# Another way to the first block's decay factors, and other queues for the first loads, in a fused scan and feed-forward kernel

## The chip, the cores and the metric

The kernel runs on one core of one Trainium2 chip. Times are device microseconds (us) of one execution of the whole kernel; the time before is 124.99 us, the median of three runs (124.52 to 125.14). The engines are PE (TensorE), DVE (VectorE), ACT (ScalarE) and POOL (GpSimd); SP (SyncE) issues transfers. Each engine takes its instructions in the order in which the program gives them. SP, ACT and POOL each have a queue of transfers (DMA).

## What is computed

A chunked linear recurrence (a state-space layer with 4 batches, 8 heads, 768 tokens, 32 channels and a state of 16) is followed by a bilinear feed-forward layer:

```python
for c in range(nc):                       # chunks of the sequence
    cum = np.cumsum(log(a)[chunk])
    L = np.exp(cum_i - cum_j) * causal    # i >= j
    M = np.einsum('bhin,bhjn->bhij', Cc, Bc) * L
    y = M @ xc + (Cc @ state) * np.exp(cum)
    state = np.exp(sum(la)) * state + sum_j(Bc xc * exp(cum_last - cum_j))
out = ((y @ w_a) * (y @ w_b)) @ w_out     # 256 -> 1536 -> 256, 3072 tokens
```

## The kernel before

**Tiling.** The sequence is cut into 6 blocks of 128 tokens, and the 4 batches into 2 groups of 2 (`bt` counts the batches in a group), so there are 12 pairs of block and group; pair `p` is block `p // 2`, group `p % 2`. In the first four pairs a partition holds two neighbouring tokens (64 partitions for each of the two batches); later pairs hold one token on each partition. For a pair, B and C are scaled by decay factors (`scale_bc`, tiles bm and cm), turned by PE (`transposes`), multiplied into scores (`scores`), masked by `causal` (`mask`, L426), multiplied with x (`pv_u`, `pv`) and then sent through the feed-forward units: PE multiplies by Wa and Wb into the banks aps and bps, ACT copies aps to asb (L639), DVE multiplies bps by asb into hk (L646), and PE multiplies hk by Wo (ops).

**The decay factors.** `a` lies in `a_sb` on 32 partitions (batch and head) by block and token. `scan` (L234) runs a product along the 128 tokens of a block into Pr. The factor of a token is that product over the product at the block's middle, token 63: `over_mid` (L238) takes the reciprocal of the middle into rmid. C is scaled by the factor and B by its inverse. For block 0 `first_factors` (L241) scales Pr by rmid into Pe and turns it, 32 partitions by 64 columns at a time, into fC on 128 partitions, four turns; f0 (L761) takes the reciprocal into fB, and the scaling of B and C of pair 0 follows on DVE (L763, L764). The factors of the other blocks come later and in other ways. The products at the ends of the blocks (`hr`, L830, from Pr and rmid) carry the state from block to block.

**The order.** It is written out by hand (`manual_schedule`): the order of the calls is the order on each engine and each queue. At the start:

- SP issues a (L183), then B of pair 0's first batch, half of the C of that batch, the small table ch, half of the x of that batch, x of pair 1's first batch (x1), and the table c32. x1 is made to wait for f0 (L762).
- ACT issues B and C of pair 0's second batch, the other half of the first batch's C, x of the second batch and the other half of the first batch's x; behind these it loads its function table (L195).
- POOL clears the tile warm (L196), makes ident by a select (L205), makes both halves of causal by a select each (L208 to L212), and then issues B and C of pair 1 (four transfers), the first halves of Wa (two transfers), x of pair 1's second batch, and the first halves of Wb (two transfers). Its next work is the scaling of B and C of pair 1 (L778, L783), and then the second halves of Wa and Wb.
- DVE sets constants with memsets, waits for a, and makes the factors.
- PE runs multiplications without use (`warmup`) until the first transposes.

PE's first feed-forward units come at L801 (Wa) and L823 (Wb); the masks of pair 1 lie between them, pv of pair 1 after the first four matmuls with Wb. `times(0, 0)` (L829) is the first product into hk; hr, hs and hsx (L830 to L837) stand between it and `times(0, 1)`.

Of the kernel before, what the change touches and what calls it, by code (L numbers as in the profile page):

```python
# [10 lines left out]
f32 = mybir.dt.float32  # L11
# [3 lines left out]
ALU = mybir.AluOpType  # L15
# [14 lines left out]
def kernel(  # L30
# [13 lines left out]
    nc = tc.nc  # L44

    nb, H, S, D = x.shape
    N = B.shape[-1]
    Q = 128
# [5 lines left out]
    BH = nb * H  # L54
    NBP = nb // 2
    NP = NBP * NBLK
    NG = NBLK - 1
# [19 lines left out]
    causal = const.tile([128, 2, Q], f16, name="causal")  # L77
# [5 lines left out]
    big = ctx.enter_context(tc.tile_pool(name="big", bufs=1))  # L83
    a_sb = big.tile([BH, NBLK, Q], f32, name="a_sb")
    zero = big.tile([BH, Q], f32, name="zero")
# [11 lines left out]
    Pr = big.tile([BH, NBLK, Q], f32, name="Pr")  # L97
    rmid = big.tile([BH, NBLK], f32, name="rmid")
    NE = P0 // NBP
    fB = big.tile([128, NE, 2, NBP, H], f32, name="fB")  # L100
    fC = big.tile([128, NE, H + 4 * NBP * H], f32, name="fC")
    Pe = big.tile([BH, 2, 64], f32, name="Pe")
    selr = big.tile([BH, 2, NBP, H], f32, name="selr")
    NL = NBLK - P0 // NBP
    Ps = big.tile([BH, NL, Q], f32, name="Ps")
# [2 lines left out]
    hr = big.tile([BH, NG], f32, name="hr")  # L108
# [34 lines left out]
    def by_token(t_):  # L143
        return t_.rearrange("p h r n -> p (h r n)").rearrange("p (t h n) -> p t h n", t=2, h=H)

    def load1(eng, p, which, bt, i0=0, n=64):
        blk, bp = divmod(p, NBP)
        if p >= P0:
            return eng.dma_start(
                by_token(pair_in[p][which])[:, bt],  # L150
                (B, C, x)[which][2 * bp + bt, :, blk * Q : (blk + 1) * Q, :].rearrange("h q n -> q h n"),
            )
        src = (B, C, x)[which][2 * bp + bt, :, blk * Q + 2 * i0 : blk * Q + 2 * i0 + 2 * n, :]
        return eng.dma_start(
            pair_in[p][which][64 * bt + i0 : 64 * bt + i0 + n].rearrange("i h r n -> i h (r n)"),
            src.rearrange("h (i r) n -> i h (r n)", r=2),
        )
# [10 lines left out]
    def load_w(W, t, f=None):  # L168
        src = (moe_w_a if W is Wa else moe_w_b).rearrange("(f p) e -> p f e", p=128)[:, :, t * KC : (t + 1) * KC]
        fs = slice(0, 2) if f is None else slice(f, f + 1)  # L170
        return nc.gpsimd.dma_start(W[t][:, fs], src[:, fs])
# [12 lines left out]
    for p_ in range(3):  # L184
        tiles(p_)
    load1(nc.scalar, 0, 0, 1)
    load1(nc.sync, 0, 0, 0)
    load1(nc.scalar, 0, 1, 1)
    load1(nc.sync, 0, 1, 0, 0, 32)
    nc.sync.dma_start(ch, ph_t.ap())  # L190
    load1(nc.scalar, 0, 1, 0, 32, 32)
    load1(nc.scalar, 0, 2, 1)
    load1(nc.sync, 0, 2, 0, 0, 32)
    load1(nc.scalar, 0, 2, 0, 32, 32)
    nc.scalar.preload_act_table_set("natural_log_exp_and_others")  # L195
    nc.gpsimd.memset(warm.bitcast(u32), 0)  # L196
    nc.vector.memset(ident, 1.0)
    nc.vector.memset(causal, 1.0)
    nc.vector.memset(zero, 0.0)
    nc.vector.memset(hsx, 0.0)  # L200
    nc.vector.memset(causal_q, 1.0)
    nc.vector.memset(c32, 0.0)
    x1 = load1(nc.sync, 1, 2, 0)
    nc.sync.dma_start(c32[0:BH], p32_t.ap())
    nc.gpsimd.affine_select(  # L205
        out=ident, in_=ident, compare_op=ALU.is_equal, fill=0.0, base=0, pattern=[[-1, 128]], channel_multiplier=1
    )
    for bt in range(2):  # L208
        v = causal[64 * bt : 64 * bt + 64]
        nc.gpsimd.affine_select(  # L210
            out=v, in_=v, compare_op=ALU.is_ge, fill=0.0, base=0, pattern=[[-1, 2], [1, Q]], channel_multiplier=-2
        )  # L212
    for w in range(2):
        for bt in range(2):
            load1(nc.gpsimd, 1, w, bt)
    load_w(Wa, 0, 0)
    load_w(Wa, 0, 1)
    load1(nc.gpsimd, 1, 2, 1)
# [3 lines left out]
    def warmup(n, bank, reps=4):  # L222
        for _ in range(n):
            nc.tensor.matmul(
                bank[:, 0 : 128 * reps],
                warm,
                warm.unsqueeze(1).broadcast_to((128, reps, 128)),
                start=True,
                stop=True,
                skip_group_check=True,  # L230
            )


    def scan(lo, hi):  # L234
        for k in range(lo, hi):
            nc.vector.tensor_tensor_scan(Pr[:, k], a_sb[:, k], zero, 1.0, ALU.mult, ALU.add)

    def over_mid(lo, hi):  # L238
        nc.vector.reciprocal(rmid[:, lo:hi], Pr[:, lo:hi, 63])

    def first_factors():  # L241
        nc.vector.tensor_scalar(Pe, Pr[:, 0].rearrange("p (i r) -> p r i", r=2), rmid[:, 0:1], None, ALU.mult)
        for bt in range(2):
            for c in range(2):
                p0 = 64 * bt + 32 * c
                nc.vector.transpose(  # L246
                    fC[p0 : p0 + 32, 0, H - H * bt : H - H * bt + 64], Pe[:, :, 32 * c : 32 * c + 32]
                )

    def second_sel():  # L250
        nc.vector.tensor_scalar(
# [390 lines left out]
    def times(p, k2, b_ps, asb):  # L642
        s = st[p]
        if "hk" not in s:
            s["hk"] = ffh.tile([128, NK, 2 * Q], f16, name="hk", tag="hk")
        nc.vector.tensor_tensor(  # L646
            out=s["hk"][:, 2 * k2 : 2 * k2 + 2, :].rearrange("p k q -> p (k q)"), in0=b_ps, in1=asb, op=ALU.mult
        )
# [104 lines left out]
    def pull(p):  # L753
# [1 line left out]
            st[p].update(st.pop(("S", p)))  # L755

    warmup(11, SC[3])
    scan(0, 1)
    over_mid(0, 1)
    first_factors()  # L760
    f0 = nc.vector.reciprocal(fB[:, 0, :, 0], f_c(0)[:, :, 0])  # L761
    tc.add_manual_dep(x1.ins, f0.ins.name, AFTER, reason="x of pair 1 behind x of pair 0")  # L762
# [24 lines left out]
        out=causal_q, in_=causal_q, compare_op=ALU.is_ge, fill=0.0, base=0, pattern=[[1, Q]], channel_multiplier=-1  # L787
# [30 lines left out]
    for bt in range(2):  # L818
# [8 lines left out]
    units_mm(0, range(3), Wb, bps, 1, range(6))  # L827
    nc.scalar.copy(maskbd, headm.unsqueeze(2).broadcast_to((128, H, D)))
    times(0, 0, bps[0], asb[0])  # L829
    nc.vector.tensor_tensor(out=hr, in0=Pr[:, 0:NG, Q - 1], in1=rmid[:, 0:NG], op=ALU.mult)  # L830
    nc.vector.tensor_tensor(out=hs, in0=hr, in1=Pr[:, 1:NBLK, 63], op=ALU.mult)
    nc.vector.tensor_tensor(
        out=hsx[0:BH],
        in0=hs.unsqueeze(1).broadcast_to((BH, nb, NG)),
        in1=selb.rearrange("p (b g) -> p b g", b=nb),
        op=ALU.mult,
# [243 lines left out]
```

## Time and profile before

| What | Value |
|---|---|
| median of three runs | 124.99 us (124.52 to 125.14) |
| the profiled execution | 125.11 us |
| its span, first to last instruction | 123.4 us |
| PE busy | 117.3 us (95%) |
| DVE busy | 91.0 us (74%) |
| ACT busy | 75.7 us (61%) |
| POOL busy | 61.2 us (50%) |
| granted clock of PE | 1.000 |

The transfers at the start, by issue and time to landing (from the answers of the trace for short stretches; B, C and x of a pair come in one transfer for each batch, 64 KB for B and C and 128 KB for x, or in halves of these):

| Transfer | Queue | Issued at, us | Landed after, us |
|---|---|---|---|
| a | SP | 0.79 | 2.1 |
| B of pair 0, second batch | ACT | 0.79 | 2.5 |
| B of pair 0, first batch | SP | 1.24 | 3.0 |
| C of pair 0, second batch | ACT | 1.54 | 3.1 |
| C of pair 0, first batch, half | SP | 2.01 | 2.9 |
| B of pair 1, first batch | POOL | 2.21 | 3.3 |
| ch | SP | 2.65 | 3.0 |
| x of pair 0, second batch | ACT | 2.93 | 4.6 |
| B of pair 1, second batch | POOL | 3.08 | 3.7 |
| x of pair 0, first batch, half | SP | 3.34 | 4.0 |
| x of pair 0, first batch, other half | ACT | 3.58 | 4.1 |
| Wa, first piece | POOL | 5.12 | 5.1 |
| x of pair 1, first batch | SP | 5.21 | 6.6 |
| c32 | SP | 5.86 | 6.1 |
| x of pair 1, second batch | POOL | 6.20 | 6.1 |
| Wb, first piece | POOL | 6.91 | 6.2 |

Busy shares are averages over the span. A chain of waits is followed back from the last instruction, at each step to what released it. A line of the timeline gives start and duration, the engine, the line of the code, what is written from what, the shapes, how many instructions are merged, and in brackets how long the engine had been idle and what ended that.

### The profile page before, as it was taken

Reading aid. Unit: us, or ns where it says so; the run is one execution under the profiler, and the core shown is the slowest. Engines: PE = TensorE matmul, PEld = TensorE weight load, DVE = VectorE, ACT = ScalarE, POOL = GpSimd, SP = SyncE. Lnnn points to the kernel's source line nnn. Section 1 sums busy time; section 2 is a strip of 40 time slices with the busy share of each in tenths; the row PEclk is TensorE's granted clock in tenths of the full one; section 3 lists DMA queues with packets and bytes.
Section 4 is the critical chain, followed back from the end, with each engine's and each line's share of the span. In section 5 each row is a group of like instructions: output and inputs, shape, how many; then the busy total and the mean of one; then the engine's idle time right before and its main releaser. Section 6 shows DMA issues by size and latency. Waiting matters only on the chain.

```text
span 123.4 us, 3704 instructions
## 1 busy us (share of the span) xinstructions
PE 117.3 (95%) x1456; PEld 80.0 (65%) x1456; DVE 91.0 (74%) x182; ACT 75.7 (61%) x158; POOL 61.2 (50%) x88
## 2 busy tenths in 40 slices
PE   6799799999999999999999999999999999999990
PEld 2345669889898798744477465757464775555890
DVE  3999598973995979799986988996889544747200
ACT  0447846837669866987669767457637746657220
POOL 7997989099492994097996970056000000000000
PEclk9999999999999999999999999999999999999999
DMA  3999999978899989799977601011101012010122
GB/s 66 195 155 210 185 198 204 164 137 77 89 125 115 108 111 103 91 118 93 129 271 169 204 5 45 5 43 45 43 0 43 5 43 88 0 48 0 43 85 85
DMA packets 56401, 12.15 MB, mean 99 GB/s; under 512 B 51168, under 2 KB 55936, under 8 KB 56384
## 3 DMA queue, kind: packets, MB, share of 16 engines
q1 hardware_dynamic: 51808, 7.43, 36.3%
q0 software_dynamic: 2304, 4.06, 17.4%
q10 hardware_dynamic: 2272, 0.43, 1.8%
q8 instruction: 11, 0.18, 0.6%
q14 instruction: 6, 0.05, 0.1%
HBM read 11.13 MB, written 3.15 MB: 116 GB/s over the span
## 4 chain that ended last, share of the span: by engine, by line
PE 85%; DMA 7%; DVE 5%; issue 1%; ACT 0%; DVEq 0%
PE ops L718 17%; PE aps L693 17%; PE bps L693 16%; PE ops L661 9%; PE aps L615 8%; PE bps L615 7%; DMA Wb<-in_moe_w_b_dram 5%; PE SC L372 2%; PE SC L432 2%; PE tr L342 2%; DMA a_sb<-in_a_dram 2%; DVE hk L646 1%; PE bps L628 1%; PE SC L447 1%; PE SC L522 1%; DVE fC L246 1%
## 5 line engine op out<-in xcount | busy, mean ns | idle before, releaser
L639 ACT COPY asb<-aps 128x512 f32<-128x512 f32 x72 | 41.9, 587 | 16.0 <-PE aps L693 10.4
L703 DVE TENSOR_TENSOR hkb<-bps,asb 128x512 f16<-128x512 f32 x48 | 32.3, 688 | 11.8 <-ACT asb L639 10.4
L693 PE MATMUL aps<-XB,Wa 128*128 128x512 f16 x96 | 28.6, 379 | 0.0
L693 PE MATMUL bps<-XB,Wb 128*128 128x512 f16 x96 | 28.5, 379 | 0.0
L718 PE MATMUL ops<-Wo,hkb 128*128 128x256 f16 (+1 forms) x204 | 22.8, 267 | 0.0
L718 PEld LDWEIGHTS <-hkb 128*128 128x128 f16 x204 | 18.4, 98 | 3.0
L426 DVE TENSOR_TENSOR t<-SC,causal_q 128x512 f16<-128x512 f32 x27 | 17.3, 681 | 2.2 <-PE SC L372 2.2
L646 DVE TENSOR_TENSOR hk<-bps,asb 128x512 f16<-128x512 f32 x24 | 15.6, 681 | 3.5 <-ACT asb L639 2.1
L693 PEld LDWEIGHTS <-Wb 128*128 128x128 f16 x96 | 9.9, 103 | 11.0 <-issue 0.2
L693 PEld LDWEIGHTS <-Wa 128*128 128x128 f16 x96 | 9.7, 104 | 9.2 <-issue 0.3
L730 ACT ACTIVATE osb<-ops 128x256 f32<-128x256 f32 (+1 forms) x16 | 6.0, 376 | 12.7 <-PE ops L718 12.6
L615 PE MATMUL bps<-X2T,Wb 128*128 128x256 f16 x84 | 12.6, 273 | 0.1
L615 PE MATMUL aps<-X2T,Wa 128*128 128x256 f16 x84 | 12.5, 273 | 0.2 <-DVE hk L646 0.2
L305 POOL TENSOR_SCALAR x<-xn 128x512 f16<-128x512 f32 x8 | 11.9, 1489 | 0.7
L661 PE MATMUL ops<-Wo,hk 128*128 128x256 f16 x96 | 11.7, 273 | 0.0
L661 PEld LDWEIGHTS <-hk 128*128 128x128 f16 x96 | 9.0, 98 | 1.2
L615 PEld LDWEIGHTS <-Wb 128*128 128x128 f16 x84 | 8.5, 103 | 1.1 <-issue 0.5
L615 PEld LDWEIGHTS <-Wa 128*128 128x128 f16 x84 | 8.4, 104 | 1.2 <-issue 0.5
L424 POOL TENSOR_TENSOR t<-tmp,causal_q 128x512 f16<-128x512 f32 x5 | 5.8, 1156 | 6.2 <-ACT tmp L423 6.1
L426 DVE TENSOR_TENSOR t<-SC,causal 128x512 f16<-128x512 f32 x13 | 8.2, 678 | 0.3 <-PE SC L387 0.2
L595 POOL TENSOR_TENSOR spair<-U,ch 128x128 f16<-128x128 f32 x8 | 3.1, 398 | 10.3 <-DVE U L579 10.3
L346 ACT ACTIVATE bt<-tr,ch 128x256 f16<-128x256 f16 x16 | 6.7, 472 | 0.5 <-PE tr L342 0.5
(101 smaller groups left out, 136.1 us busy)
## 6 DMA issues: line engine op xcount, KB each, us to landing
out_dram<-osb SPq DMA_DIRECT2D x23, 128.0 KB, 1.8
xn<-in_x_dram SPq DMA_DIRECT2D x5, 256.0 KB, 4.6
cn<-in_C_dram SPq DMA_DIRECT2D x8, 128.0 KB, 4.3
bn<-in_B_dram SPq DMA_DIRECT2D x8, 128.0 KB, 4.7
Wo<-in_moe_w_out_dram POOLq DMA_DIRECT2D x2, 384.0 KB, 5.9
xn<-in_x_dram POOLq DMA_DIRECT2D x3, 256.0 KB, 4.8
Wa<-in_moe_w_a_dram POOLq DMA_DIRECT2D x2, 192.0 KB, 5.5
xn<-in_x_dram SPq DMA_DIRECT2D x3, 128.0 KB, 3.5
```

Of the source, the lines that this page charges most:

```text
L305: eng.tensor_scalar(xo, xi, XS, None, ALU.mult)
L346: b_.append(nc.scalar.activation(out=o_, in_=TB, func=AF.Copy, scale=par[:, e : e + 1]))
L424: nc.gpsimd.tensor_tensor(out=o_, in0=tmp, in1=c_, op=ALU.mult)
L426: nc.vector.tensor_tensor(out=o_, in0=i_, in1=c_, op=ALU.mult)
L615: nc.tensor.matmul(ps[:, kk * 2 * Q : (kk + 1) * 2 * Q], w_up(W, k, f), X2T[:, p, :, f], start=(f == 0), stop=(f == 1), skip_group_check=True,
L639: (nc.vector.tensor_copy if on_dve else nc.scalar.copy)(asb, a_ps)
L646: nc.vector.tensor_tensor(out=s["hk"][:, 2 * k2 : 2 * k2 + 2, :].rearrange("p k q -> p (k q)"), in0=b_ps, in1=asb, op=ALU.mult)
L661: nc.tensor.matmul(o_ps[:, 0:d_model], hk[:, k, bt * Q : (bt + 1) * Q], Wo[:, k, :], start=(k == 0), stop=(k == NK - 1), skip_group_check= ...
L693: nc.tensor.matmul(t_, w_up(W, k, f), XB[:, blk - P0 // NBP, f].rearrange("p t j q -> p (t j q)"), start=(f == 0), stop=(f == 1), skip_gro ...
L703: return lambda: nc.vector.tensor_tensor(out=s["hk"][:, k], in0=ps[1], in1=asb, op=ALU.mult)
L718: nc.tensor.matmul(o_ps[:, 0:w], hk[:, k, c * Q : (c + 1) * Q], Wo[:, k, cs], start=(k == 0), stop=(k == NK - 1), skip_group_check=True,)
L730: nc.scalar.activation(out=o_sb[:, 0:w], in_=o_ps[:, 0:w], func=AF.Copy, scale=1.0 / (YS * YS))
```

## The change

Block 0's factors no longer come from Pr. Two scans of 64 tokens each run from the start and from the middle of the block and write Pf on 64 partitions: the first half of the tokens on partitions 0 to 31, the second on 32 to 63. The second half starts from 1 at the middle, so only the first half is divided by the product at the middle (r0, which is 1 on the other partitions). One scaling on 64 partitions and two turns of 64 partitions by 64 columns follow. The scan and the reciprocal of block 0 into Pr and rmid are gone, and hr's first column is copied from Pf.

At the start, the loads of the first batch's C and x are no longer halved and come from SP alone. C of pair 0's second batch goes from ACT to POOL, and B of pair 1's first batch from POOL to SP, ahead of x1. ACT loads its table behind its first transfer. POOL makes only the lower half of causal by a select, ahead of ident, and DVE copies it to the upper half.

```diff
@@ tiles
-    Pe = big.tile([BH, 2, 64], f32, name="Pe")
+    Pf = big.tile([64, 64], f32, name="Pf")
+    r0 = big.tile([64, 1], f32, name="r0")
+    Pe = big.tile([64, 2, 32], f32, name="Pe")
@@ start
     load1(nc.scalar, 0, 0, 1)
     load1(nc.sync, 0, 0, 0)
-    load1(nc.scalar, 0, 1, 1)
-    load1(nc.sync, 0, 1, 0, 0, 32)
+    load1(nc.sync, 0, 1, 0)
     nc.sync.dma_start(ch, ph_t.ap())
-    load1(nc.scalar, 0, 1, 0, 32, 32)
+    nc.scalar.preload_act_table_set("natural_log_exp_and_others")
     load1(nc.scalar, 0, 2, 1)
-    load1(nc.sync, 0, 2, 0, 0, 32)
-    load1(nc.scalar, 0, 2, 0, 32, 32)
-    nc.scalar.preload_act_table_set("natural_log_exp_and_others")
+    load1(nc.sync, 0, 2, 0)
+    load1(nc.sync, 1, 0, 0)
+    x1 = load1(nc.sync, 1, 2, 0)
     nc.gpsimd.memset(warm.bitcast(u32), 0)
+    nc.vector.memset(causal[0:64], 1.0)
     nc.vector.memset(ident, 1.0)
-    nc.vector.memset(causal, 1.0)
     nc.vector.memset(zero, 0.0)
+    nc.vector.memset(r0, 1.0)
...
-    x1 = load1(nc.sync, 1, 2, 0)
     nc.sync.dma_start(c32[0:BH], p32_t.ap())
+    nc.gpsimd.affine_select(
+        out=causal[0:64],
+        in_=causal[0:64],
...
+    load1(nc.gpsimd, 0, 1, 1)
     nc.gpsimd.affine_select(
         out=ident, in_=ident, compare_op=ALU.is_equal, fill=0.0, base=0, pattern=[[-1, 128]], channel_multiplier=1
     )
-    for bt in range(2):
-        v = causal[64 * bt : 64 * bt + 64]
-        nc.gpsimd.affine_select(
...
-    for w in range(2):
-        for bt in range(2):
-            load1(nc.gpsimd, 1, w, bt)
+    nc.vector.tensor_copy(causal[64:128], causal[0:64])
+    for w, bt in ((0, 1), (1, 0), (1, 1)):
+        load1(nc.gpsimd, 1, w, bt)
@@ def first_factors
-        nc.vector.tensor_scalar(Pe, Pr[:, 0].rearrange("p (i r) -> p r i", r=2), rmid[:, 0:1], None, ALU.mult)
+        for c in range(2):
+            nc.vector.tensor_tensor_scan(
+                Pf[BH * c : BH * c + BH], a_sb[:, 0, 64 * c : 64 * c + 64], zero[:, 0:64], 1.0, ALU.mult, ALU.add
+            )
+        nc.vector.reciprocal(r0[0:BH], Pf[0:BH, 63:64])
+        nc.vector.tensor_scalar(Pe, Pf.rearrange("p (i r) -> p r i", r=2), r0, None, ALU.mult)
         for bt in range(2):
-            for c in range(2):
-                p0 = 64 * bt + 32 * c
-                nc.vector.transpose(
-                    fC[p0 : p0 + 32, 0, H - H * bt : H - H * bt + 64], Pe[:, :, 32 * c : 32 * c + 32]
-                )
+            c0 = H - H * bt
+            nc.vector.transpose(fC[64 * bt : 64 * bt + 64, 0, c0 : c0 + 64], Pe)
@@ main
     warmup(11, SC[3])
-    scan(0, 1)
-    over_mid(0, 1)
     first_factors()
...
     times(0, 0, bps[0], asb[0])
-    nc.vector.tensor_tensor(out=hr, in0=Pr[:, 0:NG, Q - 1], in1=rmid[:, 0:NG], op=ALU.mult)
+    nc.vector.tensor_copy(hr[:, 0:1], Pf[BH : 2 * BH, 63:64])
+    nc.vector.tensor_tensor(out=hr[:, 1:], in0=Pr[:, 1:NG, Q - 1], in1=rmid[:, 1:NG], op=ALU.mult)
```

## The prediction

> **What bounds the kernel now.** I read the busy shares first: PE 117.3 us of a span of 123.4, so wherever the other engines keep it fed, the end is set by PE. Next the chain that ended last, in order of time. Its columns are start, duration and piece of work:
>
> ```profile
> 0.79 2.09 DMA a_sb<-in_a_dram
> ...
> 5.22 0.43 DVE bm L316
> 6.36 0.44 DVE ct L358
> 6.91 6.16 DMA Wb<-in_moe_w_b_dram
> 13.12 0.62 PE bps L628 x4
> 14.39 0.56 PE bps L628 x4
> 15.05 0.69 DVE hk L646
> 16.12 0.69 DVE hk L646
> 16.85 0.60 PE aps L615 x4
> ```
>
> From 16.85 us on the pieces are nearly all PE work laid end to end. Everything that the change touches lies ahead of that, so its worth is the shift of the 16.85. The chain has two stretches there. Up to about 6.9 it is the preparation of pair 0 (a, the factors, B and C). Then the transfer of the first Wb half takes over: issued at 6.91, landed at 13.07, used at 13.12. What PE waited for says how loose the first stretch is:
>
> ```profile
> PE bps L628 <- DMA Wb<-in_moe_w_b_dram: 0.7, 1, 0.7
> ```
>
> If the preparation were earlier and Wb were not, PE would wait longer at the same place: this wait of 0.71 us is already there. So **the preparation has slack and the weights' landing decides**. The timeline of DVE at the start, the part that is rewritten:
>
> ```profile
> 2.98 0.41 DVE L236 TENSOR_TENSOR_SCAN Pr<-a_sb,zero 32x128 f32<-32x128 f32 x1 [1.19 <-DMA a_sb<-in_a_dram]
> 3.42 0.15 DVE L239 RECIPROCAL rmid<-Pr 32x1 f32<-32x1 f32 x1
> 3.61 0.27 DVE L242 TENSOR_SCALAR Pe<-Pr,rmid 32x128 f32<-32x128 f32 x1
> 3.92 0.98 DVE L246 STREAM_TRANSPOSE fC<-Pe 32x64 f32<-32x64 f32 x4
> 4.93 0.25 DVE L761 RECIPROCAL fB<-fC 128x16 f32<-128x16 f32 x1
> 5.22 0.42 DVE L316 TENSOR_TENSOR bm<-bn,fB 128x256 f16<-128x256 f32 x1
> ```
>
> And the busy time by stretches of 1 us (the last two columns: share of the DMA engines that is busy, GB/s). It shows transfers short of saturated up to 4 us and saturated after:
>
> ```profile
> 2.00:3.00 1.00, 1.00 (x4) 0.30 (x2) 0.03 (x1) 0.00 (x0) 1.00 (x2) 1.00 0.70 141
> 3.00:4.00 1.00, 1.00 (x4) 0.34 (x3) 0.90 (x4) 0.00 (x0) 1.00 (x3) 1.00 0.70 110
> 4.00:5.00 1.00, 1.00 (x5) 0.31 (x3) 0.93 (x5) 0.76 (x1) 1.00 (x2) 1.00 1.03 209
> ...
> 12.00:13.00 1.00, 0.41 (x4) 0.12 (x2) 1.00 (x3) 0.99 (x2) 1.00 (x2) 1.00 1.23 157
> ```
>
> **The factors.** Before, scan to the reciprocal fB takes 2.98 to 4.93, 1.95 us: 0.41 + 0.15 + 0.27 + 0.98, and 0.14 of gaps. The two scans of 64 columns are not in the trace. Above, they cost the 0.71 of the pair of full scans at 10.16; below, half of that, 0.36. I take 0.46, because a DVE instruction on one column costs 0.15 and that part is not halved. The scaling, 64 columns instead of 128, lies between the 0.23 of L251 (32 columns) and 0.27: 0.25. The two turns handle 64 partitions by 64 columns; the four old ones took 0.245 each on 32 by 64. If the length of a row sets the time, two cost 0.49; if both halves are done one after the other, 0.98. DVE's rows here go by columns (a reciprocal of 128x16 costs 0.25, hardly more than 32x1), so 0.49. The sum is 0.46 + 0.15 + 0.25 + 0.49 + 0.14 = 1.49: **0.46 us earlier**, with ends of 0.58 earlier (0.36 + 0.15 + 0.23 + 0.49 + 0.14 = 1.37) and 0.30 later (0.71 + 0.15 + 0.27 + 0.98 + 0.14 = 2.25).
>
> What is late next: bm could start at 4.76 and cm at 5.10. C's half of pair 0 now comes by POOL. Its queue holds, ahead of it, the clearing of warm and one causal select that waits for a DVE memset (0.27, from 0.89) and takes 0.44: issue at about 1.6. Loads of this kind from POOL land 3.3 to 3.7 us after issue, so at 4.9 to 5.3. ch, on SP behind a C load that is now whole, landed at 5.65 and is wanted by the copy of bt (6.03 before, 5.57 then); that gives back about 0.2. So the preparation comes 0.25 to 0.45 earlier, and by the paragraph above this alone is worth nothing.
>
> **The queues.** POOL before: three selects (to 2.27), four loads of B and C of pair 1 from 2.21 (0.87, then three at 0.70), Wa at 5.12. After: one select to 1.63, C's load (0.87), the select of ident (0.29), three loads (2.10): Wa's issue at 1.6 + 0.87 + 0.29 + 2.1 = 4.86, and everything behind it, the x of pair 1 and Wb among it, **0.26 earlier**. POOL carries as many loads ahead of Wa as before.
>
> ACT issues five loads before (0.79 to 4.21) and two after. Its table load (1.28, at 4.24 before) moves into ACT's idle time, and x of pair 0 follows it at about 2.8 against 2.93; if issuing does not wait for the table load, at 1.55. SP gets the whole half of C (0.60 to 0.72), the whole half of x (0.60, landing about 4.6 after issue as ACT's does) and B of pair 1 (0.72) ahead of x of pair 1, which still waits for f0: at 5.21 before, now at about 4.8.
>
> **The landing of Wb.** The bytes ahead of it stay. Transfers reach full use only at 4 us; the two stretches at 0.70 hide 0.6 us that could be won if the same loads were handed over sooner. So Wb lands between 0 (all by bytes) and 0.85 earlier (0.26 of issue and 0.6 of filled time). The bounds are far apart; the issue row is the nearest, with part of the filling, so I take **0.40**. The wait at 13.12 is then shorter than the preparation's slack, which moves as well, so all 0.40 passes.
>
> **Additions.** The copy into hr is new, between the first two hk (15.05 and 16.12), where DVE is on the chain. Rows: hr itself, 0.14, of which 0.07 is on the chain; hs, 0.17 with its gap. So 0.05 to 0.18, and I take **0.10**. The half copy of causal on DVE costs at most the 0.43 of a 128x256 copy of f16 and lies in the 1.19 us in which DVE waits for a; without that cover it would delay the scan by its length. The memset of r0 costs about what that of hsx does, 0.08, in the same cover; one select less takes 0.43 from POOL, counted above.
>
> **Sum:** -0.40 + 0.10 = -0.30. The profiled execution took 125.11 (span 123.4 and 1.7 around it), giving 124.8; the median shown, 124.99, is 0.12 lower than that execution, so the forecast is **124.7 us**.
>
> **A rule that speaks against it.** The row: POOL's issues take 0.69 to 0.70 each from 3.08 to 5.12 while DVE is 0.90 to 0.93 busy, so I see no lock. The Trainium skill, "SBUF — State Buffer", in the passage on the "DVE blocks DMA" trap, says that a transfer issued by GpSimd can't have its descriptors written while DVE runs a copy in a two-port mode, and it gives about 620 ns growing to 3100 ns. By this rule of the Trainium skill the causal copy could hold up C's load, and the sum would be that of the late C below; by the row it stays 124.7.
>
> **Rivals.**
>
> *The idle transfer time is filled whole.* For it: x of pair 0 may be issued under the table load, POOL starts its loads 0.6 us sooner, and the 0.70 rows show the room. Against it: SP has more to issue than before. Wb 0.75 earlier, less 0.10: 124.99 - 0.65 = 124.3.
>
> *B of pair 1 starves on SP's queue, and the kernel is slower.* It stands behind the whole half of x and meets the weights from POOL. The row that speaks for it: x of pair 1 on SP, issued at 5.21, landed 6.6 us later at 11.8, 4.1 us after x of pair 0 (7.68). B has half its bytes in as many runs, so it would need 2.05 to 4.1 us behind x: landing at 9.7 instead of in time for POOL's scaling at 8.11. Bm, cm, the transposes on PE and the masks of pair 1 then move by 1.6; PE takes its work in order, and pv of pair 1, at 13.66 with the masks done at 12.96, has 0.70 of slack. The loss is 1.6 - 0.7 = 0.9, so 125.9. It decides from a landing of 8.8 on. Against it: ACT's queue is emptier, so SP's gets a larger share; with even shares B lands at about 8.
>
> *C's half by POOL is late.* POOL's loads of B and C land 3.3 to 5.3 us after issue, so at 6.9 in the worst row. Then cm starts at 6.9 instead of 5.56; 1.34 less the 0.71 of slack, and the 0.10: +0.7, 125.7. The lock that the Trainium skill describes would act here.
>
> *Nothing but the copy.* Wb's landing goes by bytes: 125.1.
>
> **How the numbers follow.** Forecast 0.40 (Wb 0.1 to 0.75 earlier and the copy 0.05 to 0.18: 124.3 to 125.1), filled whole 0.28, starved B 0.18, late C 0.05, nothing 0.09. About 0.5%, 0.62 us, is what a measurement of this kernel can tell from no change, as the three runs spread over 0.62: faster means below 124.37, slower above 125.61. Faster: 0.10 of the forecast and 0.20 of the second, 0.30. Slower: 0.16 of the starved B and 0.04 of the late C, 0.20. The rest, 0.50, is the same. The range reaches from 123.9 (Wb 0.85 earlier, no cost for the copy, and part of the preparation's gain) to 125.9, the starved B.
>
> **What would show it.** In the profile after: two turns at about 0.25 and f0 near 4.45; Wa issued near 4.86; Wb landed near 12.7 and PE's wait for it still there; hr's copy at about 0.1; the first bps of L615 0.3 earlier. I am wrong if POOL's scaling of pair 1 waits for bn, if cm waits for cn, or if Wb lands where it did.

## The result, and the profile after

| | before | after |
|---|---|---|
| median of 15 runs, us | 124.99 (124.52 to 125.37) | 125.51 (125.27 to 128.25) |
| after over before | | 1.0058, 95% interval 1.0036 to 1.0081 |
| the profiled execution, us | 125.11 | 125.92 |
| its span, us | 123.4 | 124.2 |

The kernel became 0.5 us slower. Ratios, here and below, are worked out without the executions over 1.5% longer than the fastest of their kernel, and medians from all of them, so a ratio is not the quotient of two medians. The profiled execution of the changed kernel lies 0.4 us above its median, so its profile shows the loss larger than it usually is. DVE's part at the start, in the timeline after (start, duration, engine and line, what is written from what; in brackets the idle time before and what ended it):

```profile
2.88 0.59 DVE L249 TENSOR_TENSOR_SCAN Pf<-a_sb,zero 32x64 f32<-32x64 f32 x2 [0.81 <-DMA a_sb<-in_a_dram]
3.51 0.15 DVE L252 RECIPROCAL r<-Pf 32x1 f32<-32x1 f32 x1
3.69 0.45 DVE L253 TENSOR_SCALAR Pe<-Pf,r 64x64 f32<-64x64 f32 x1
4.18 0.49 DVE L256 STREAM_TRANSPOSE fC<-Pe 64x64 f32<-64x64 f32 x2
4.70 0.25 DVE L767 RECIPROCAL fB<-fC 128x16 f32<-128x16 f32 x1
4.99 0.42 DVE L324 TENSOR_TENSOR bm<-bn,fB 128x256 f16<-128x256 f32 x1
6.50 0.42 DVE L324 TENSOR_TENSOR cm<-cn,fC 128x256 f16<-128x256 f32 x1 [1.09 <-DMA cn<-in_C_dram]
```

The factors are ready earlier (bm at 4.99 against 5.22), and then cm waits 1.09 us for C. Before, cm ran at 5.56 without a wait. The masks of pair 0, which began at 7.42 before, begin at 8.30. The two halves of C landed 4.3 us (POOL) and 4.4 us (SP) after issue. The chain that ended last, in order of time:

```profile
3.97 5.52 DMA bn<-in_B_dram
...
9.66 0.61 POOL bm L324
...
14.17 0.42 PE SC L455 x32
...
16.91 0.69 DVE hk L654
17.60 0.04 issue
17.64 0.60 PE aps L623 x4
```

It now runs through B of pair 1, which SP issued at 3.97. The `aps` that stood at 16.85 stands at 17.64, 0.79 us later, and the executions differ by 0.81: nearly the whole loss is there by then. Wb is no longer on the chain, but it did not land earlier: issued at 6.60 instead of 6.91, it took 6.5 us instead of 6.2. The stretches of 1 us show the transfers (last two columns: busy share of the DMA engines, GB/s):

```profile
3.00:4.00 1.00, 1.00 (x4) 0.40 (x3) 0.90 (x4) 0.00 (x0) 1.00 (x2) 1.00 0.89 186
4.00:5.00 1.00, 0.84 (x4) 0.20 (x2) 0.88 (x5) 0.00 (x0) 1.00 (x3) 1.00 1.21 188
5.00:6.00 1.00, 0.40 (x3) 0.17 (x3) 0.41 (x1) 0.00 (x0) 1.00 (x3) 1.00 1.11 148
6.00:7.00 1.00, 0.02 (x1) 0.02 (x2) 0.50 (x2) 0.16 (x1) 1.00 (x2) 1.00 1.22 132
```

and two of the same stretches before:

```profile
5.00:6.00 1.00, 0.34 (x4) 0.17 (x3) 0.96 (x4) 0.52 (x1) 1.00 (x3) 1.00 1.11 253
6.00:7.00 1.00, 0.79 (x23) 0.47 (x30) 0.84 (x4) 0.84 (x2) 1.00 (x3) 1.00 1.14 145
```

The idle share of 3 to 4 us was filled as hoped (0.89 against 0.70, 186 GB/s against 110). But from 5 to 7 us engines that are at least as busy as before move 148 and 132 GB/s instead of 253 and 145. Something made the transfers longer, and that is what the experiments had to find.

### The profile page after: what moved, and what is told of

It reads as the page before. It is cut to its first block, busy times and chain, and to the rows that moved or that the text cites. A ratio compares the mean times of both kernels' runs of the same rounds, so it can differ in the third digit from the quotient of the medians.

```text
span 124.2 us, 3703 instructions
## 1 busy us (share of the span) xinstructions
PE 116.5 (94%) x1456; PEld 80.0 (64%) x1456; DVE 91.4 (74%) x184; ACT 75.7 (61%) x158; POOL 60.8 (49%) x87
## 3 DMA queue, kind: packets, MB, share of 16 engines
q1 hardware_dynamic: 52848, 7.60, 41.7%
## 4 chain that ended last, share of the span: by engine, by line
PE 85%; DMA 4%; DVE 4%; SPq 2%; POOL 1%; issue 1%; ACT 0%; POOLq 0%
PE ops L726 17%; PE aps L701 17%; PE bps L701 16%; PE ops L669 9%; PE aps L623 8%; PE bps L623 8%; DMA bn<-in_B_dram 4%; PE SC L380 2%; DVE t L434 2%; PE SC L440 2%; PE tr L350 2%; SPq L156 2%; PE SC L455 1%; PE SC L530 1%; PE bps L636 1%
## 5 line engine op out<-in xcount | busy, mean ns | idle before, releaser
L647 ACT COPY asb<-aps 128x512 f32<-128x512 f32 x72 | 41.9, 587 | 15.6 <-PE aps L701 10.3
L701 PE MATMUL bps<-XB,Wb 128*128 128x512 f16 x96 | 28.5, 379 | 0.0
L654 DVE TENSOR_TENSOR hk<-bps,asb 128x512 f16<-128x512 f32 x24 | 15.6, 680 | 2.9 <-ACT asb L647 2.3
L738 ACT ACTIVATE osb<-ops 128x256 f32<-128x256 f32 (+1 forms) x16 | 6.0, 376 | 12.7 <-PE ops L726 12.6
L623 PE MATMUL bps<-X2T,Wb 128*128 128x256 f16 x84 | 12.4, 272 | 0.0
```

Of the source, the lines that this page charges most:

```text
L623: nc.tensor.matmul(ps[:, kk * 2 * Q : (kk + 1) * 2 * Q], w_up(W, k, f), X2T[:, p, :, f], start=(f == 0), stop=(f == 1), skip_group_check=True,
L647: (nc.vector.tensor_copy if on_dve else nc.scalar.copy)(asb, a_ps)
L654: nc.vector.tensor_tensor(out=s["hk"][:, 2 * k2 : 2 * k2 + 2, :].rearrange("p k q -> p (k q)"), in0=b_ps, in1=asb, op=ALU.mult)
L701: nc.tensor.matmul(t_, w_up(W, k, f), XB[:, blk - P0 // NBP, f].rearrange("p t j q -> p (t j q)"), start=(f == 0), stop=(f == 1), skip_gro ...
L738: nc.scalar.activation(out=o_sb[:, 0:w], in_=o_ps[:, 0:w], func=AF.Copy, scale=1.0 / (YS * YS))
```

## The experiments

Each set ran on one chip beside the kernel before; each ratio is to the kernel before in the same set.

| Run | What it is | Median, us (before) | Ratio, 95% interval | SP's queue, share |
|---|---|---|---|---|
| | changed kernel, first measurement | 125.51 (124.99) | 1.0058, 1.0036 to 1.0081 | 41.7% |
| e1 | before + factors | 125.01 (124.83) | 0.9998, 0.9974 to 1.0021 | 43.2% |
| e2 | before + loads and queues | 124.93 (124.83) | 1.0016, 0.9990 to 1.0042 | 37.0% |
| e3 | changed, hr, hs, hsx early | 124.81 (124.83) | 0.9997, 0.9973 to 1.0021 | 43.2% |
| e4 | before, hr, hs, hsx early | 124.77 (124.83) | 0.9996, 0.9973 to 1.0018 | 36.3% |
| r5 | changed, again | 125.45 (124.80) | 1.0041, 1.0023 to 1.0058 | 44.7% |
| r6 | changed, B of pair 1 on POOL | 125.47 (124.80) | 1.0051, 1.0031 to 1.0070 | 44.1% |
| r7 | changed, x of pair 0 held back | 126.87 (124.80) | 1.0066, 1.0031 to 1.0101 | 40.9% |
| r8 | changed, hr's copy early | 125.32 (124.80) | 1.0037, 1.0013 to 1.0061 | 42.8% |
| s1 | before, tiles moved by 32 bytes | 125.19 (124.75) | 1.0031, 1.0006 to 1.0056 | 42.1% |
| s2 | changed, tiles moved back | 124.96 (124.75) | 1.0017, 0.9997 to 1.0036 | 37.1% |
| s3 | s2, hr, hs, hsx early | 124.95 (124.75) | 1.0010, 0.9988 to 1.0032 | 37.2% |
| s4 | before + factors, tiles in place, hr, hs, hsx early | 124.43 (124.75) | 0.9967, 0.9947 to 0.9986 | 36.6% |
| t3 | changed, offset 32 | 125.50 (124.81) | 1.0031, 1.0013 to 1.0050 | 42.5% |
| t1 | changed, offset 64 | 125.40 (124.81) | 1.0034, 1.0015 to 1.0053 | 38.0% |
| t2 | changed, offset 128 | 125.17 (124.81) | 1.0012, 0.9995 to 1.0029 | 37.3% |
| t4 | changed, offset 0 | 125.02 (124.81) | 1.0015, 0.9993 to 1.0038 | 36.9% |

**One part alone (e1, e2), and DVE's stretch (e3, e4).** The first theory was that the order of the loads made the loss, with the copy into hr as a second part. e1 and e2 take one half of the change each; e3 and e4 move these lines ahead of the first product into hk:

```diff
-    times(0, 0, bps[0], asb[0])
     nc.vector.tensor_copy(hr[:, 0:1], Pf[BH : 2 * BH, 63:64])     # e3 only
     nc.vector.tensor_tensor(out=hr[:, 1:], ...)
     nc.vector.tensor_tensor(out=hs, ...)
     nc.vector.tensor_tensor(out=hsx[0:BH], ...)
+    times(0, 0, bps[0], asb[0])
```

> The kernel before with the new factors alone (scans of 64 on 64 partitions, two turns, the copy into hr); loads, queues and selects as before. Theory (the loads make the loss): the preparation of pair 0 is 0.2 to 0.45 us earlier (bm near 4.99 as in the changed kernel, cm right behind it), Wb lands at 13.1 as before, PE's wait for it grows by about as much, and the stretch between the first two hk is 1.37 as in the changed kernel instead of 1.07: 0.3 us slower, 125.3. Rival 1 (the copy into hr and the factors make the whole loss): 0.5 to 0.8 slower. Rival 2 (the preparation is worth something): not slower than before.

> The kernel before with the new loads, queues, selects and table load, but the old factors. Theory (the loads make the loss): cm waits for cn until about 6.5, pair 1's bm waits for bn until about 9.5, the first hk starts at about 15.5 instead of 15.05, the stretch between the first two hk stays 1.07: 0.5 us slower, 125.5. Rival 1 (hr's copy makes the loss): no change, 125.0.

> The changed kernel with the four instructions for hr, hs and hsx put ahead of the first product into hk instead of behind it. Theory: they then lie in DVE's idle time before the first hk (0.58 us, so nearly all of their 0.64), the second hk follows the first at once and the loss shrinks by 0.3 to 0.6 us: 125.0 to 125.2. Rival (PE's bps or asb ends last there, not DVE): no change.

> The kernel before with the same move of hr, hs and hsx. DVE was idle for 1.25 us ahead of the first hk, so the 0.38 us between the first two hk disappears: 0.2 to 0.4 us faster than before, 124.6 to 124.8. Rival (the pieces behind are held by PE, whose weights came late): no change.

Neither half alone is measurably slower, so the theory lost its simplest form. With e2's loads alone, cm ran at 5.67, 0.09 us behind bm, and pair 1's bm at 7.70 without a wait for a transfer, although its first dozen transfers were issued within 0.05 us of the changed kernel's. The same issues, and C some 0.8 us earlier (its last part landed at 5.6 instead of 6.4): the order of the loads by itself was not what made C late. With e1's factors alone, and the loads as before, C's last part landed at 5.5 (5.0 in e4, which has the same loads), so cm waited, and ch was late too:

```profile
5.60 0.43 DVE L321 TENSOR_TENSOR cm<-cn,fC 128x256 f16<-128x256 f32 x1 [0.36 <-DMA cn<-in_C_dram]
6.25 0.84 ACT L351 ACTIVATE bt<-tb,ch 128x256 f16<-128x256 f16 x2 [0.75 <-DMA ch<-ph]
```

e3 is as fast as before, although its cm waited 0.74 us for C; e4 is no faster.

**The changed kernel again, and one repair at a time (r5 to r8).** r6 and r7 each undo or hold one load, r8 moves the copy alone:

```diff
# r6
-    load1(nc.sync, 1, 0, 0)
-    for w, bt in ((0, 1), (1, 0), (1, 1)):
+    for w, bt in ((0, 0), (0, 1), (1, 0), (1, 1)):
         load1(nc.gpsimd, 1, w, bt)
# r7
-    load1(nc.scalar, 0, 2, 1)
+    x01 = load1(nc.scalar, 0, 2, 1)
...
-        nc.vector.reciprocal(r0[0:BH], Pf[0:BH, 63:64])
+        rr = nc.vector.reciprocal(r0[0:BH], Pf[0:BH, 63:64])
+        tc.add_manual_dep(x01.ins, rr.ins.name, AFTER, reason="x of pair 0 behind C of pair 0")
# r8
     over_mid(2, NBLK)
+    nc.vector.tensor_copy(hr[:, 0:1], Pf[BH : 2 * BH, 63:64])
```

> The changed kernel once more, beside the kernel before, as the measure for the next three. Theory (late C and B of pair 0 and 1, and the longer stretch between the first two hk): again 0.4 to 0.9 us slower than before, about 125.4; cm waits for cn, pair 1's bm waits for bn past 8.9. Rival (the loss belongs to the chip of the first measurement): within 0.2 us of before.

> The changed kernel with B of pair 1's first batch back on POOL's queue, ahead of the second batch, and off SP's. Theory: pair 1's bm starts by 8.5 and waits for no transfer, cm of pair 0 is still late, the first hk starts 0.4 us earlier than in the changed kernel and the time falls by 0.3 to 0.5 us, to about 125.0. Rival (late C of pair 0 alone decides, or hr's stretch): no change against the changed kernel.

> The changed kernel with x of pair 0's second batch made to wait for the reciprocal r0 (about 3.65), so that it is issued behind C instead of at 1.56. Theory: cm's wait for cn shrinks from 1.1 to under 0.3 and the masks of pair 0 start about 0.8 earlier, but B of pair 1 still comes from SP behind x and stays late, so the time falls by no more than 0.2 us. Rival (late C decides): the time falls by 0.5 us to that of the kernel before.

> The changed kernel with the copy into hr alone moved to DVE's idle time behind the reciprocals of the later blocks; hr, hs and hsx stay. Theory: the stretch between the first two hk falls from 1.37 to 1.07 or 1.2 and the time by 0.15 to 0.3 us. Rival (PE is held there by something else): the stretch shrinks and the time does not.

r5 confirms the loss in another set. r6 speaks against the starved B as its cause: bm of pair 1 ran at 8.37 with no wait for a transfer, and the time stayed. (r6 also issues Wa and Wb 0.68 us later than r5, as POOL has one more load ahead of them; Wb landed at 12.6 in both.) The masks of pair 0 start at 8.20 in r5 and 8.19 in r6, because cm waits for C in both, and DVE is busy from there through the masks of pair 1 with hardly a gap. r7 brought C in time (cm at 5.38, no wait) with the tiles where the change puts them, and was no faster for it; its runs spread from 124.99 to 128.46. In its profile PE waits for Wb and ACT for x:

```profile
PE bps L637 <- DMA Wb<-in_moe_w_b_dram: 1.1, 1, 1.1
```

So x held back is x late, and the expected gain did not come. r8 shortened the stretch between the first two hk to 1.07 us, as before the change, and its median fell by 0.13 us, less than the measurement tells, which is what its rival said.

**The place of the tiles (s1 to s4).** What e1 and the changed kernel share, and e2 does not, is the new tile r0. It has one column, takes 32 bytes of each partition, and moves every tile allocated behind it, B, C, x and the outputs among them. Before, these start at a multiple of 256 bytes in a partition (the first B at 73,472 = 287 x 256); after, 32 bytes past one. (The weights' tiles lie ahead of r0, 32 bytes past a multiple of 256 in every kernel here.) The share of SP's queue over the span (q1 in the page; ACT's transfers are in q10) follows that: 36.3 to 37.2% in the seven profiles with the tiles in place, 40.9 to 44.7% in the nine with them 32 bytes off.

```diff
# s1, on the kernel before
+    pad = big.tile([64, 1], f32, name="pad")
...
+    nc.vector.memset(pad, 1.0)
# s2, on the changed kernel (t1: 16, t2: 32, t3: 8, t4: 64 columns)
-    r0 = big.tile([64, 1], f32, name="r0")
+    r0 = big.tile([64, 64], f32, name="r0")[:, 0:1]
```

> The kernel before with one more tile of a single column (it takes 32 bytes of each partition, as r0 does in the changed kernel) and a memset of it; nothing else is changed, but the tiles of B, C, x and of the outputs now start 32 bytes past a multiple of 256 in a partition, as in the changed kernel, instead of at a multiple. New theory (the place of the tiles makes SP's transfers slower): the share of SP's queue over the span rises from 36.3% to 41 to 45%, the loads of pair 0 and 1 land 0.3 to 0.8 us later, the time rises by 0.1 to 0.5 us. Rival (the order of the loads alone): share and time as before.

> The changed kernel with r0 the first column of a tile of 64 columns, so that the tiles behind it start at multiples of 256 bytes again. New theory: SP's queue has a share of 36 to 38% again, cm waits for cn under 0.3 us (0.65 to 1.09 in five profiles of the changed loads and factors), x of pair 0 lands near 7.1 and the time falls by 0.3 to 0.5 us against the changed kernel, to 124.9 to 125.1; the longer stretch between the first two hk stays. Rival (the order of the loads alone makes C late): cm waits for 0.6 or more and the time stays at 125.45.

> As the one before, and the four instructions for hr, hs and hsx put ahead of the first product into hk. New theory: both losses are undone and the preparation is 0.25 us earlier: 0.2 to 0.5 us faster than the kernel before, 124.3 to 124.6. Rival (the weights' landing or PE's next instructions hold it): as the kernel before within 0.15 us.

> The kernel before with the new factors alone, r0 in 64 columns, and hr, hs and hsx ahead of the first product into hk; loads and queues as before. New theory: SP's queue at 36 to 37%, bm near 4.8 and cm right behind it, 0.1 to 0.4 us faster than before. Rival: as the kernel before.

s1 changes addresses and adds one memset in DVE's idle time, nothing else, and it is slower by 0.31% (0.06 to 0.56). Its profiled execution (125.03) is not longer than that of the kernel before (125.11), so through which wait s1 loses is not seen. From the page of s1, the row of q1 (packets, MB, share of 16 engines):

```profile
q1 hardware_dynamic: 51808, 7.43, 42.1%
```

and the same row of the kernel before:

```profile
q1 hardware_dynamic: 51808, 7.43, 36.3%
```

The same packets and bytes take 16% more of the engines' time (42.1 / 36.3). x of pair 0 landed at 8.2 instead of 7.6. s2, the changed kernel with its tiles back in place, lands both halves of C by 5.4 and x by 7.0:

```profile
5.50 0.43 DVE L324 TENSOR_TENSOR cm<-cn,fC 128x256 f16<-128x256 f32 x1
```

Its cm no longer waits. s4, the factors alone with both repairs, is the only run that is faster than before, by 0.33% (0.14 to 0.53). e4, which has the move of hr, hs and hsx without the factors, is not, but it ran in another set and the two intervals overlap; and in s4, as in e1, C's last part landed at 5.5 to 5.6 and cm waited (0.29 us). So with the loads as before C's landing does not follow the place, and what the factors add in s4 is not shown. s3 adds the new loads to s4 and loses 0.4% of it again; the two intervals, of one set, do not overlap. s3 is also no faster than e3, the same kernel with the tiles 32 bytes off (1.0010 and 0.9997, in two sets): there the place brought nothing that the measurement tells.

**Which boundary (t1 to t4).**

> The changed kernel with r0 in a tile of 16 columns: the tiles of B, C, x and the outputs start 64 bytes past a multiple of 256. If any 256-byte boundary counts, for runs of 128 bytes (B, C) 64 is as bad as 32: SP's queue 41 to 45%, cm waits for cn by 0.6 us or more, 125.4. If only a multiple of 64 counts, SP's queue 36 to 38% and 125.0.

> As the one before with 32 columns: 128 bytes past a multiple of 256. Runs of 128 bytes then cross no boundary of 256, runs of 256 bytes (x of the first pairs) and of 1024 (the outputs) do. If boundaries of 256 count, SP's queue lies between, 37 to 41%, and C of pair 0 is in time; if a multiple of 64 or 128 is enough, 36 to 38%.

> As the ones before with 8 columns, which gives the changed kernel's own offset of 32 bytes: the reference of this set. SP's queue 41 to 45%, cm waits for cn by 0.6 us or more, 0.3 to 0.7 us slower than before.

> As the ones before with 64 columns: offset 0, beside the 32 in the same set. SP's queue 36 to 38%; if the place of the tiles is most of the loss, 0.3 to 0.5 us faster than the offset of 32 and within 0.25 us of the kernel before; if it is less than half, still 0.4 us or more slower than before.

SP's queue between 2 and 8 us, where B, C and x of the first pairs are loaded (packets, MB, share of 16 engines); offset 32 (t3):

```profile
q1 hardware_dynamic: 2296, 0.39, 54.9%
```

offset 64 (t1):

```profile
q1 hardware_dynamic: 2302, 0.39, 49.5%
```

offset 128 (t2):

```profile
q1 hardware_dynamic: 2342, 0.40, 37.3%
```

offset 0 (t4):

```profile
q1 hardware_dynamic: 2336, 0.40, 35.8%
```

A packet took 23.0 ns at offset 32 (0.549 x 6 us x 16 / 2296), 20.6 at 64, 15.3 at 128 and 14.7 at 0. These loads write runs of 128 bytes (B, C) and 256 bytes (x). At 128 they cost what they cost at 0, at 64 nearly what they cost at 32. The later pairs' B and C come in runs of 64 bytes, and over the whole span offset 64 costs little (38.0%) where 32 costs much (42.5%). All this fits one reading: a run is slow when, by its start, it touches one more line of 128 bytes than its length needs. The start alone is not enough, though. ACT's queue, which in the same window loads B and x of pair 0's second batch into tiles that are moved as well, took 16.6 to 16.7% for 1056 packets at all four offsets; and between 2 and 4 us SP's queue took 16 ns a packet at offset 32 as at 0 (28.9% for 572 packets, 28.5% for 566). Between 6 and 8 us it was 27 against 14 (57.6% for 672, 21.6% for 495). The difference begins at about 4 us, when POOL's transfers join (4.3% of the engines' time from 2 to 4 us, 39.5% from 4 to 6, in t3); whether it needs them, and why, is open.

In time, offset 0 was 0.48 us below offset 32 by the medians of one set (125.02 and 125.50), and 0.21 us of the loss stays; the ratios, 1.0015 and 1.0031, have intervals that overlap, so the split is known only roughly. One of t2's twelve executions took 299.1 us; why is not known.

**Which piece decides.** The prediction read off the trace that the worth of the change is the shift of the `aps` at 16.85. That holds in every profile: the time of the execution is 108.1 to 108.4 us after the start of this piece in sixteen of the eighteen, 108.5 and 108.7 in e3 and e4. In twelve it starts 0.72 to 0.74 us after the second hk starts on DVE; in six (e2, s1, s3, s4, t2, t4) it starts later, because PE stopped ahead of it for no wait that the profile names (the last section). From the timelines:

| Profile | Second hk, us | This aps, us | Execution, us |
|---|---|---|---|
| before | 16.12 | 16.85 | 125.11 |
| changed kernel | 16.91 | 17.64 | 125.92 |
| r5, changed kernel again | 16.48 | 17.21 | 125.45 |
| s2, tiles in place | 15.70 | 16.43 | 124.66 |
| t4, tiles in place | 15.68 | 16.98 (stop) | 125.23 |
| e3, hr, hs, hsx early | 15.61 | 16.34 | 124.81 |
| s3, both | 14.83 | 16.00 (stop) | 124.25 |

So two delays come together ahead of the second hk: the late C, which pushes the masks, and the longer stretch behind the first hk. In these profiles either repair alone brings the second hk back to 15.6 or 15.7, ahead of the kernel before, and beyond that PE's stop can take over. This may be why s3's median is no lower than e3's; the rows are of one execution each, so it is not shown.

## Why the prediction was wrong

I forecast 124.7 us and no change or a gain; it is 125.51. The piece to watch, the `aps` at 16.85, was right; what sets it was wrong. All three signs of being wrong that I named took place: cm waited for cn (1.09 us), POOL's scaling of pair 1 waited for bn (landed at 9.49), and Wb landed where it did.

**The step that failed: durations of transfers were carried over from the trace of before** ("Loads of this kind from POOL land 3.3 to 3.7 us after issue, so at 4.9 to 5.3"). They held for tiles at multiples of 256 bytes. The diff adds r0, I priced its memset (0.08 us), and I did not ask where the tiles behind it go. The halves of C landed at 5.9 and 6.4 us, and the masks of pair 0 began 0.88 us later than before instead of a little earlier. With the place alone put back (s2) they landed at 5.2 and 5.4, inside or near the forecast's range. The place had help: ACT issued x of pair 0 at 1.56, under its table load, where I had taken 2.8, and with this x held to 3.68 (r7) C landed at 4.9 and 5.3 although the tiles lay 32 bytes off.

**The weights' landing did not decide in the changed kernel.** The wait of 0.71 us for Wb, on which the sum rests, belongs to one execution: in e4, with the same loads, Wb landed at 12.4 and PE did not wait for it. In the changed kernel the second hk on DVE decided. In the profiled execution the first hk began 0.49 us later than before (15.54 and 15.05) and the second another 0.30, together the 0.79; in r5 it was 0.07 and 0.29.

**Wb 0.40 earlier: 0.** It landed at 13.1 as before. Its issue was 0.31 earlier (0.26 predicted) and the idle time was filled, so both parts of the term took place, and brought nothing. That the longer transfers took them back is not shown: with the loads of before Wb landed at 12.4 in e4 and at 12.2 in s1, whose tiles are 32 bytes off, and with the new ones at 12.0 to 12.8 in place (s2, s3, t2, t4) and at 12.6 to 13.1 off it (r5, t3, the changed kernel). Single executions differ by 0.7 us here.

**The copy into hr: 0.10 predicted, 0.30 measured.** The stretch between the first two hk in the changed kernel:

```profile
15.54 0.69 DVE L654 TENSOR_TENSOR hk<-bps,asb 128x512 f16<-128x512 f32 x1 [0.58 <-ACT X2T L518]
16.27 0.14 DVE L836 COPY hr<-Pf 32x1 f32<-32x1 f32 x1
16.44 0.15 DVE L837 TENSOR_TENSOR hr<-Pr,rmid 32x4 f32<-32x4 f32 x1
16.63 0.15 DVE L838 TENSOR_TENSOR hs<-hr,Pr 32x5 f32<-32x5 f32 x1
16.82 0.17 DVE L839 TENSOR_TENSOR hsx<-hs,c 32x20 f32<-32x20 f32 x1
16.91 1.27 DVE L654 TENSOR_TENSOR hk<-bps,asb 128x512 f16<-128x512 f32 x2
```

and before:

```profile
15.05 0.69 DVE L646 TENSOR_TENSOR hk<-bps,asb 128x512 f16<-128x512 f32 x1 [1.25 <-PE bps L628]
15.65 0.14 DVE L830 TENSOR_TENSOR hr<-Pr,rmid 32x5 f32<-32x5 f32 x1
```

The old hr began 0.09 us before the first hk's end; the copy begins 0.04 after it, and the product behind it waits for the copy: 0.17 for the copy's slot and 0.13 for the lost overlap. The stretch is 1.37 us against 1.07. In the profiles of the changed kernel all of it reaches the aps, which starts 0.73 us after the second hk. In the times it is less clear: r8 took the copy away without a measurable gain, and e3, which moves three more instructions out of the stretch, was as fast as before, in another set than r5.

**The factors: 0.46 earlier predicted, 0.23 measured** at bm, and 0.41 in e1 (4.81). Of the 0.23 the scan's earlier start (2.88 and 2.98, as a landed sooner) gave 0.10; from the scan to the reciprocal it took 1.82 us, and 1.62 in e1, instead of 1.49. The turns took 0.49 as worked out (the row that I gave for it, 0.25 against 0.15, hardly shows it, so this was in part luck); the two scans took 0.59 instead of 0.46, and the scaling 0.45 in the changed kernel and 0.25 in e1. That the preparation by itself is worth nothing is not refuted: e1, with its tiles off their place, is as fast as before, and in s4 cm ran at 5.67, not ahead of the 5.56 of before.

**The rivals.** Both slower ones took place in the profile. The late C, given 0.05, came near its rival's figure, cm at 6.50 where I had put it at 6.9; r6 and s2 fit it, while in e3 the late C (cm at 6.19) cost nothing that the measurement tells, with DVE's stretch cleared. The starved B, given 0.18 and priced at 0.9 us, shows in the profiled execution (bn landed 5.5 us after issue, at 9.49), but in r6 it was gone and nothing was won. I had put both down to the queue; the place of the tiles was the part that I did not see. The new loads cost something beside that (s3 against s4); through which wait stays open, since the profile of s3 is of one of its fastest executions (124.25, median 124.95) and shows no late load.

## What to carry to other kernels

A new tile moves every tile that is allocated behind it. After any change of allocations compare the queues' shares at equal packet and byte counts: SP's rose here from 36.3% to 42.1% by the place alone, and showed in one profile what the time shows only in many runs. Give small tiles whole multiples of 128 bytes, or allocate them last. And find the piece behind which everything keeps its distance, and read in every profile what started it: here the second hk or PE's stop, and the repairs of two delays ahead of it did not add up in the times (e3, s2 and s3).

## What the hardware showed that I had not expected

**Runs that do not start on a line of 128 bytes.** Between 2 and 8 us a packet of SP's queue took 23.0 ns at offset 32, 20.6 at 64, 15.3 at 128 and 14.7 at 0, while ACT's took the same at all four. The Trainium skill, "DMA: Bandwidth & Descriptors", in the section on how a descriptor splits into AXI transactions, says of reads that a transaction starts at a 256-byte boundary and that a descriptor off it costs more beats. The runs agree that the start counts, but 128 past a multiple of 256 cost next to nothing here; for these writes into SBUF the boundary that fits the measurements is 128, and the cost showed only from about 4 us on, with POOL's transfers beside them.

**PE waits for its own instructions.** In many profiles PE stops at the same place, behind the first matmul of pair 1 with Wb, for no wait that the profile names, as here in t4:

```profile
16.63 0.51 PE L623 MATMUL bps<-X2T,Wb 128*128 128x256 f16 x3 [1.31 <-issue]
```

The queue of instructions carries one packet of 0.02 MB ahead of it. In the ten profiles with the stop, PE goes on 2.2 to 2.5 us after that packet's start (13.8 and 16.18 in the kernel before, 14.4 and 16.63 in t4); in the others the packet started at 12.3 to 13.5 and there is no such stop. In none of the eighteen does PE pass this place sooner than 2.2 us after the packet's start. The start moves by 2 us between executions without a relation to PE's progress that I could see, and this gate caps what earlier weights are worth: e2 was 0.7 us ahead of the kernel before at its first hk (14.38 and 15.05) and its span was 0.2 us longer (123.6 and 123.4). The Trainium skill, "Runtime: NRT & Kernel Launch", in the section on instruction fetch mechanics, describes an instruction memory refilled in blocks of 16 KiB by the sequencer's own queue and calls the cost mostly hidden; here, with the transfer engines full (1.17 and 1.15 from 14 to 16 us in t4), the stop was up to 1.3 us. That the stop is this refill is inferred from the times; no run moved the packet.

**DVE's scaling beside POOL's issue.** With the new loads and factors the scaling into Pe ended at 4.14 to 4.18 in all twelve profiles, whether it began at 3.68 or at 3.93 (0.25 to 0.47 us long), near the end of one of POOL's issues (4.12 to 4.14); with the old loads it took 0.24 to 0.25 in e1 and s4. The Trainium skill, "SBUF — State Buffer", in the section on SBUF's two separate sides, says that of DVE in a two-port mode and GpSimd the later one blocks. I had looked for that in POOL's issues, where no row showed it; here it may have been DVE that waited, which was not tested and cost nothing in the changed kernel, since cm waited longer for C.
